# Keys a step ahead of queries in the attention stage of a Performer and mixture-of-experts kernel

## The chip, the cores and the metric

The kernel runs on one core of a Trainium2 chip. The metric is the device time of one execution in microseconds. Engines are named as in the profile: PE (TensorE; PEld is its loading of weights), DVE (VectorE), ACT (ScalarE), POOL (GpSimd), and SP, whose queue issues DMAs.

## The reference

Three layers in a row. The first is Performer attention over 2 batches, 8 heads, 576 positions and 64 dimensions with 128 random features; its output, 1152 rows of 512, goes through four experts, and then through `h * cos(h)` between two matrices. The change lies in the first:

```python
def phi(x):
    proj = np.einsum('bhsd,md->bhsm', x, omega)
    sq = np.sum(x * x, axis=-1, keepdims=True) / 2.0
    h = proj - sq
    h = h - np.max(h, axis=-1, keepdims=True)
    return np.exp(h) / np.sqrt(m)
q_p, k_p = phi(q * scale), phi(k * scale)
kv = np.einsum('bhsm,bhsd->bhmd', k_p, v)
z = np.sum(k_p, axis=2)
num = np.einsum('bhsm,bhmd->bhsd', q_p, kv)
den = np.einsum('bhsm,bhm->bhs', q_p, z)[..., None] + 1e-06
return num / den
```

## The kernel before

Attention is worked in eight steps, one for each batch and pair of heads, over the first 512 positions; the last 64 positions of all heads and both batches form a tail (`kL`, `qL`) of their own. One step `s` turns k and q (PE transposes them in `turn`, and a copy brings them back to SBUF), projects them on the features (`features`: eight matmuls `pj`, which write two banks, the two heads of the pair on the two halves of PE's rows), and takes the exponentials. The exponential's bias is minus the norm term minus the maximum. POOL squares the input and adds up to eight partial sums for each row (`norms`), DVE sums these (`sq`), takes the maximum of each of the eight projections of a row (`mx`), and forms the bias in two operations with two inputs each (`bias`, line 984). ACT applies the eight exponentials of a pair (line 1010).

Around it, `kv_of` multiplies the key features with v and adds the tail's part, `turn_phi` transposes the query features and copies them back (`pT`), `nums` multiplies them with kv and divides, and `put_x` transposes the result and splits it in a high and a low half: ACT writes the high half `xh`, DVE the low half `xl`. `kv_tail` makes the tail's part `kvL` for all heads once.

Each engine takes its instructions in the order of the program. The loop over `s` writes that order out by hand; in step `s` it is: kv of step s-1; projection of k and, in part, its bias; norms on POOL for the next k and q; transposes of the query features of s-1; bias and exponentials of k; result of s-2; projection and bias of q; transposes of the next k and q; num of s-1; loads for later steps; one piece of a weight load. The exponentials of q stand at the start of the next step. A weight unit of the expert layer is loaded in every step from 0 on, two steps later split in a high half by ACT (line 129) and a low half by POOL (line 134). From `s = 6` on, `dense_quanta` puts four quanta of six dense matmuls in a step, for the expert layer; they run on to the end of the kernel. All PSUM tiles come from one pool of eight banks.

Of the kernel before, what the change touches and what calls it, by code (L numbers as in the profile page):

```python
# [26 lines left out]
def performer_moe_kernel(ctx, tc, q, k, v, omega, probs, w1, w2, w_in, w_out, out):  # L27
# [846 lines left out]
    with tc.tile_pool(name="at1", bufs=1) as at1, tc.tile_pool(name="at2", bufs=2) as at2:  # L874
# [51 lines left out]
        ws = at1.tile([P, M], F32, name="ws")  # L926

# [8 lines left out]
        def norms(nm, t):  # L936

            x2 = at2.tile([P, 2 * R, D], F32, tag=f"x2{nm[0]}", bufs=1, name=f"x2_{nm}")
            nc.gpsimd.tensor_tensor(out=x2, in0=t, in1=t, op=ALU.mult)
            sq = at2.tile([P, 2 * R], F32, tag="sq", name=f"sq_{nm}")  # L940
            w = D
            while w > 8:
                w //= 2
                nc.gpsimd.tensor_tensor(
                    out=x2[:, :, 0:w], in0=x2[:, :, 0:w], in1=x2[:, :, w : 2 * w], op=ALU.add
                )
            yield
            nc.vector.tensor_reduce(out=sq, in_=x2[:, :, 0:w], op=ALU.add, axis=AX.X)
            yield sq

        def turn(nm, t, pieces=1):

            n = R // pieces
            tps = []
            for z in range(pieces):
                tp = bank(f"tp_{nm}_{z}")[:, : n * P]
                tps.append((slice(z * n * P, (z + 1) * n * P), tp))
                for i in range(n):
                    nc.tensor.transpose(
                        tp[:, i * P : (i + 1) * P], t[:, 2 * (z * n + i) : 2 * (z * n + i) + 2, :], ident  # L960
                    )

            def copy(x=None):
                if x is None:
                    x = at2.tile([P, R * P], F32, tag=f"xT{nm[0]}", name=f"xT_{nm}")
                for z, (c, tp) in enumerate(tps):
                    if z == (nm[0] == "q"):
# [7 lines left out]
        def features(nm, turned, phi, hold=False):  # L975

            norm = next(sqs.pop(nm))
            mx = at2.tile([P, 2 * R], F32, tag="mx", name=f"mx_{nm}")
            nb = at2.tile([P, 2 * R], F32, tag="nb", name=f"nb_{nm}")
            pjs, rs = [], []  # L980

            def bias(z):
                for dst, o in ((mx, ALU.add), (nb, ALU.subtract)):
                    nc.vector.scalar_tensor_tensor(
                        out=dst[:, z], in0=norm[:, z], scalar=-SC * SC / 2, in1=mx[:, z], op0=ALU.mult, op1=o
                    )

            pjs = [bank(f"pj_{nm}_{g}") for g in range(2)]
            for i in range(R):
                for g, pj in enumerate(pjs):  # L990
                    r = slice(g * D, (g + 1) * D)
                    nc.tensor.matmul(
                        pj[:, i * M : (i + 1) * M], turned[r, i * P : (i + 1) * P], ws[r, :], start=True, stop=True
                    )
            for g, pj in enumerate(pjs):
                rs.append(slice(g, 2 * R, 2))
                nc.vector.tensor_reduce(
                    out=mx[:, rs[-1]], in_=pj.rearrange("p (a m) -> p a m", m=M), op=ALU.max, axis=AX.X
                )
                if nm in ("kL",) and not g:  # L1000
                    bias(rs[-1])

            if hold:
                yield
            bias(rs[-1] if nm in ("kL",) else slice(0, 2 * R))
# [51 lines left out]
        def kv_tail(phi):  # L1057
            for hp in range(NP):
# [6 lines left out]
                nc.scalar.activation(kvL[hp].rearrange("p h b e -> p h (b e)"), kvp, ACTF.Copy)  # L1065
# [15 lines left out]
        def turn_phi(i):  # L1081
            phq = phqs[i]
            for h in range(2):
# [4 lines left out]
                if h == 0:  # L1088
# [65 lines left out]
        def load(i):  # L1154
            b, hp = pairs[i]
            kts[i] = load_pair(k, b, hp, "kt")
            qts[i] = load_pair(q, b, hp, "qt")

        load(0)
        load_tail(halves(kL), k)  # L1160
        load(1)
        load_v(0)
        load_tail([veL[b * L : (b + 1) * L, :, b, 0:D] for b in range(B)], v)
# [23 lines left out]
        def norms_ahead(nm, t):  # L1187
            sqs[nm] = norms(nm, t)
            next(sqs[nm])

        DQ = 1.0
        wload = []
        norms_ahead("k0", kts[0])
        norms_ahead("q0", qts[0])
        fk = fq = iter(())
        turned = {}

        def turn_ahead(s):
            splits = []
            if s == 0:  # L1200
                omega_pairs()
            if s < NPR and ("k", s) not in turned:
                splits.append(("k", turn(f"k{s}", kts[s], 2 if s == 0 else 1)))
            if s == 0:
                warm(1)
            splits.append(("q", turn(f"q{s}", qL if s == NPR else qts[s])))
            if s == 0:
                warm(1)
            for x, split in splits:
                turned[x, s] = split()  # L1210

        def query_features(s):
            phqs[s] = at1.tile([P, 2 * R, M], F32, tag="phq", name=f"phq_{s}")
            steps = features(f"q{s}", turned.pop(("q", s)), phqs[s])
            next(steps)
            return steps

        turn_ahead(0)

        xkL = at1.tile([P, R * P], F32, tag="phq", name="xkL")  # L1220
        for s in range(NPR + 3):
            for _ in fq:
                pass
            if s < first:
                advance(wload)
            dense_quanta(s, DQ)
            kvs = kv_of(s - 1) if 1 <= s <= NPR else iter(())
            next(kvs, None)
            if s != 1:
                next(kvs, None)  # L1230
            if s >= first:
                advance(wload)
            dense_quanta(s, DQ)
            fk = iter(())
            if s < NPR:
                phks[s] = at1.tile([P, 2 * R, M], F32, tag="phk", name=f"phk_{s}")
                fk = features(f"k{s}", turned.pop(("k", s)), phks[s], 1 <= s < first)
                next(fk)
            if s == 0:

                turned["kL"] = turn("kL", kL)(xkL)
                fq = query_features(0)
                norms_ahead("kL", kL)
                k1 = turn("k1", kts[1])
                for _ in fk:
                    pass
                turned["k", 1] = k1()
                phiL = at1.tile([P, H, M], F32, name="phiL")
                fL = features("kL", turned.pop("kL"), phiL)
                next(fL)  # L1250
            if s == 1:
                turn_phi(0)
                kv_tail(phiL)
                next(kvs, None)
            if s + 1 < NPR:
                norms_ahead(f"k{s + 1}", kts[s + 1])
            if s < NPR:
                norms_ahead(f"q{s + 1}", qL if s + 1 == NPR else qts[s + 1])
            dense_quanta(s, DQ)
            if not 1 <= s < first:  # L1260
                next(fk, None)
            if 2 <= s <= NPR:
                turn_phi(s - 1)
            elif s == NPR + 1:
                tail_turn_phi()
            for _ in fk:
                pass
            px = iter(())
            if 2 <= s <= NPR + 1:
                b, hp = pairs[s - 2]  # L1270
                px = put_x(f"{s - 2}", hp, xss.pop(s - 2), b * R, R)
            elif s == NPR + 2:
                px = tail_put_x()
            next(px, None)
            if s == 0:
                for _ in fq:
                    pass
            else:
                fq = query_features(s) if s <= NPR else iter(())
            for _ in px:  # L1280
                pass
            dense_quanta(s, DQ)
            if s < NPR:
                turn_ahead(s + 1)
            if s == 0:
                for _ in fL:
                    pass
            if 1 <= s <= NPR:
                nums(s - 1)
            elif s == NPR + 1:  # L1290
                tail_nums()
            if s + 2 < NPR:
                load(s + 2)
            if s + 1 < NPR:
                load_v(s + 1)
# [51 lines left out]
```

## Time and profile before

| | |
|---|---|
| median of 3 runs | 656.53 us (656.46 to 657.21) |
| the profiled execution | 656.99 us |
| its span, first to last instruction | 655.2 us |
| busy in the span: PE, DVE, ACT, POOL | 648.6, 492.9, 356.8, 173.7 us |
| attention's first eight steps begin, and its last transposes lie | from 6 to 103 us |

The span is what the trace covers; the rest of the execution's time lies around it. PE's matmuls are pipelined and their ends modelled, so the rows of PEld show better when PE goes on. Rows of the timeline merge equal instructions that follow each other; the difference of two starts tells more than a duration, because an instruction may start before the one ahead has ended.

### The profile page before, as it was taken

Reading aid. Unit: us, or ns where it says so; the run is one execution under the profiler, and the core shown is the slowest. Engines: PE = TensorE matmul, PEld = TensorE weight load, DVE = VectorE, ACT = ScalarE, POOL = GpSimd, SP = SyncE. Lnnn points to the kernel's source line nnn. Section 1 sums busy time; section 2 is a strip of 40 time slices with the busy share of each in tenths; the row PEclk is TensorE's granted clock in tenths of the full one; section 3 lists DMA queues with packets and bytes.
Section 4 is the critical chain, followed back from the end, with each engine's and each line's share of the span. In section 5 each row is a group of like instructions: output and inputs, shape, how many; then the busy total and the mean of one; then the engine's idle time right before and its main releaser. Section 6 shows DMA issues by size and latency. Waiting matters only on the chain. (4 is left out here: it accounts for less than half of the span.)

```text
span 655.2 us, 9580 instructions
## 1 busy us (share of the span) xinstructions
PE 648.6 (99%) x3479; PEld 561.1 (86%) x3479; DVE 492.9 (75%) x898; ACT 356.8 (54%) x708; POOL 173.7 (27%) x223
## 2 busy tenths in 40 slices
PE   8999999999999999999999999999999999999997
PEld 7999998998888888888888888788999888888887
DVE  5897749778879778679788587699688677596842
ACT  5887664436544555254544344464476874467921
POOL 8898451203332222333333222320000000000000
PEclk9999999999999999999999999999999999999999
DMA  7753121323544534345543255410811001700111
GB/s 185 221 155 105 34 65 32 97 65 113 154 141 156 176 113 145 128 133 164 187 129 128 99 159 178 144 59 8 319 34 34 1 0 39 284 1 2 48 49 49
DMA packets 55439, 70.93 MB, mean 108 GB/s; under 512 B 15200, under 2 KB 40032, under 8 KB 55392
## 3 DMA queue, kind: packets, MB, share of 16 engines
q1 hardware_dynamic: 46800, 40.92, 20.6%
q0 software_dynamic: 8448, 29.37, 12.9%
q8 instruction: 27, 0.44, 0.3%
q14 instruction: 20, 0.16, 0.1%
q10 hardware_dynamic: 144, 0.03, 0.0%
HBM read 55.36 MB, written 14.94 MB: 107 GB/s over the span
## 5 line engine op out<-in xcount | busy, mean ns | idle before, releaser
L674 ACT ACTIVATE sth<-h 128x512 fp32r<-128x512 f32 (+1 forms) x114 | 61.2, 551 | 69.0 <-PE g L704 54.1
L248 POOL TENSOR_TENSOR c<-c 128x512 uint32<-128x512 uint32 x32 | 47.1, 1472 | 86.6 <-issue 36.3
L677 DVE SCALAR_TENSOR_TENSOR stl<-h,sth 128x512 fp32r<-128x512 f32 (+1 forms) x72 | 49.1, 701 | 25.1 <-ACT sth L674 24.7
L704 PE MATMUL g<-v2h,sth 128*128 128x512 f32 (+1 forms) x110 | 42.6, 387 | 0.4 <-ACT sth L674 0.4
L704 PE MATMUL g<-v3h,sth 128*128 128x512 f32 (+1 forms) x110 | 42.9, 390 | 0.0
L704 PE MATMUL g<-v1h,sth 128*128 128x512 f32 (+1 forms) x110 | 42.7, 388 | 0.0
L704 PE MATMUL g<-v0h,sth 128*128 128x512 f32 (+1 forms) x110 | 42.6, 387 | 0.0
L704 PE MATMUL g<-v0h,stl 128*128 128x512 f32 (+1 forms) x110 | 42.6, 387 | 0.0
L704 PE MATMUL g<-v2h,stl 128*128 128x512 f32 (+1 forms) x110 | 42.5, 387 | 0.0
L704 PE MATMUL g<-v3h,stl 128*128 128x512 f32 (+1 forms) x110 | 42.4, 386 | 0.0
L704 PE MATMUL g<-v1h,stl 128*128 128x512 f32 (+1 forms) x110 | 42.4, 386 | 0.0
L704 PE MATMUL g<-v0l,sth 128*128 128x512 f32 (+1 forms) x110 | 42.4, 385 | 0.0
L704 PE MATMUL g<-v1l,sth 128*128 128x512 f32 (+1 forms) x110 | 42.4, 385 | 0.0
L704 PE MATMUL g<-v3l,sth 128*128 128x512 f32 (+1 forms) x110 | 42.4, 385 | 0.0
L704 PE MATMUL g<-v2l,sth 128*128 128x512 f32 (+1 forms) x110 | 42.4, 385 | 0.0
L282 DVE TENSOR_TENSOR stl<-h,sth 128x512 fp32r<-128x512 f32 (+1 forms) x42 | 24.4, 588 | 21.1 <-ACT sth L674 20.7
L403 DVE SCALAR_TENSOR_TENSOR c<-c 128x384 f32<-128x384 f32 (+2 forms) x44 | 25.8, 590 | 9.0 <-ACT c L401 8.8
L233 ACT ACTIVATE c<-c 128x512 f32<-128x512 f32 x32 | 21.1, 659 | 15.6 <-DMA kv_0h<-c 6.5
L401 ACT ACTIVATE c<-c 128x384 f32<-128x384 f32 (+2 forms) x44 | 24.4, 555 | 1.4
L704 PEld LDWEIGHTS g<-v2h,sth 128*128 128x128 f32 x110 | 20.7, 188 | 4.8 <-ACT sth L674 0.8
L704 PEld LDWEIGHTS g<-v0h,stl 128*128 128x128 f32 x110 | 20.7, 188 | 4.8 <-DVE stl L677 0.4
L704 PEld LDWEIGHTS g<-v2h,stl 128*128 128x128 f32 x110 | 20.7, 188 | 4.6 <-DVE stl L677 0.4
(415 smaller groups left out, 1930.5 us busy)
## 6 DMA issues: line engine op xcount, KB each, us to landing
rv<-in_moe_w_dram SPq DMA_DIRECT2D x16, 512.0 KB, 3.9
c<-in_moe_w_in_dram POOLq DMA_DIRECT2D x16, 512.0 KB, 4.2
c<-in_moe_w_out_dram POOLq DMA_DIRECT2D x16, 512.0 KB, 3.9
kt<-in_k_dram SPq DMA_DIRECT2D x8, 256.0 KB, 3.8
qt<-in_q_dram SPq DMA_DIRECT2D x8, 256.0 KB, 3.7
ve<-in_v_dram SPq DMA_DIRECT2D x16, 128.0 KB, 2.6
ra_2as<-in_moe_w_dram SPq DMA_DIRECT2D x8, 256.0 KB, 2.9
ra_3as<-in_moe_w_dram SPq DMA_DIRECT2D x8, 256.0 KB, 3.7
```

The lines of the kernel that those rows point to most:

```text
L233: nc.scalar.activation(t.bitcast(F32), hw.bitcast(F32), ACTF.Abs)
L248: nc.gpsimd.tensor_tensor(out=total, in0=t, in1=lw, op=ALU.add)
L282: nc.vector.tensor_tensor(out=dst, in0=x, in1=y, op=ALU.subtract)
L401: nc.scalar.activation(kk, vv, ACTF.Copy, bias=ROUND)
L403: nc.vector.scalar_tensor_tensor(out=vv, in0=kk, scalar=ROUND, in1=vv, op0=ALU.subtract, op1=ALU.subtract)
L674: nc.scalar.activation(hi, src, ACTF.Relu if self.e < E else ACTF.Copy)
L677: nc.vector.scalar_tensor_tensor(out=to, in0=src, scalar=0.0, in1=hi.bitcast(F32), op0=ALU.max, op1=ALU.subtract)
L704: nc.tensor.matmul(g, x, y[:, o : o + w], start=n == 0, stop=n == 3 * FT - 1)
```

## The change

The order of the loop changes: in step `s` the queries of `s` and the keys of `s+1` are projected one after the other, then both biases are formed, then both exponentials taken, and the next q and the k after it are turned. So keys run a step ahead; k is loaded three steps ahead, q two. The start is written out by hand for k0, q0, the tail's keys, k1, and the loop's step 0 only loads. The bias is formed by operations with one input: a sum over the eight partial norms, its scaling into a plane of a small tile `three`, the maxima into another, and two sums over the planes. For the tail's keys the norm is no longer POOL's and DVE's: ACT writes the squares beside the copy of the turned keys, and eight further matmuls add them, times a constant, into the projection, so that the negated maximum is the bias. Some copies pass from ACT to DVE (`kvL`, `pT` of step 0, one turned k). Buffers: two for `phk` and for the norms' `x2`; `xkL` and `x2L` use the places of `pT`.

```diff
-        def norms(nm, t):
+        def norms_ahead(nm, t):
...
-            yield
-            nc.vector.tensor_reduce(out=sq, in_=x2[:, :, 0:w], op=ALU.add, axis=AX.X)
-            yield sq
+            sqs[nm] = x2[:, :, 0:w]
...
+                    if x2 is not None:
+                        nc.scalar.activation(x2[:, c], tp, ACTF.Square)
...
-            def bias(z):
-                for dst, o in ((mx, ALU.add), (nb, ALU.subtract)):
-                    nc.vector.scalar_tensor_tensor(
-                        out=dst[:, z], in0=norm[:, z], scalar=-SC * SC / 2, in1=mx[:, z], op0=ALU.mult, op1=o
-                    )
...
+                for z, (x_, y) in enumerate([(turned, ws)] + [(squares, minus_norm)] * (squares is not None)):
+                    for g, pj in enumerate(pjs):
+                        r = slice(g * D, (g + 1) * D)
+                        nc.tensor.matmul(
+                            pj[:, i * M : (i + 1) * M], x_[r, c], y[r, :],
+                            start=z == 0, stop=z == (squares is not None),
+                        )
+            yield
+            three = at2.tile([P, 2 * R, 3], F32, tag=f"th{nm[0]}", name=f"three_{nm}")
+            if squares is None:
+                nc.vector.tensor_reduce(out=nb, in_=sqs.pop(nm), op=ALU.add, axis=AX.X)
+                nc.vector.tensor_scalar(
+                    out=three[:, :, 1], in0=nb, scalar1=-SC * SC / 2, scalar2=None, op0=ALU.mult
+                )
             for g, pj in enumerate(pjs):
+                to = (nb if squares is not None else three[:, :, 0])[:, g : 2 * R : 2]
                 nc.vector.tensor_reduce(
+                    out=to, in_=pj.rearrange("p (a m) -> p a m", m=M), op=ALU.max, axis=AX.X,
+                    negate=squares is not None,
                 )
+            if squares is None:
+                nc.vector.tensor_reduce(
+                    out=three[:, :, 2], in_=three[:, :, 0:2], op=ALU.add, axis=AX.X, negate=True
+                )
+                nc.vector.tensor_reduce(out=nb, in_=three[:, :, 1:3], op=ALU.add, axis=AX.X)
             yield
...
-                nc.scalar.activation(kvL[hp].rearrange("p h b e -> p h (b e)"), kvp, ACTF.Copy)
+                nc.vector.tensor_copy(out=kvL[hp].rearrange("p h b e -> p h (b e)"), in_=kvp)
...
-                if h == 0:
+                if h == 0 and i:
...
+        load_k(2)
         load_tail([veL[b * L : (b + 1) * L, :, b, 0:D] for b in range(B)], v)
...
+        norms_ahead("k0", kts[0])
+        norms_ahead("q0", qts[0])
+        norms_ahead("k1", kts[1])
+        omega_pairs()
+        k0 = turn("k0", kts[0], 2)
+        warm(1)
+        q0 = turn("q0", qts[0])
+        warm(1)
+        turned["k", 0], turned["q", 0] = k0(), q0()
...
+        fk0 = k_features(0)
+        next(fk0)
+        kL_copy = turn("kL", kL)
+        next(fk0)
+        kL_copy(xkL, x2L)
+        k1 = turn("k1", kts[1])
+        for _ in fk0:
+            pass
+        turned["k", 1] = k1()
+        fq0 = q_features(0)
+        next(fq0)
+        fL = features("kL", xkL, phiL, x2L)
+        next(fL)
+        next(fq0)
+        next(fL)
+        norms_ahead("q1", qts[1])
+        norms_ahead("k2", kts[2])
+        turn_ahead(1, act=False)
+        fk1 = k_features(1)
+        next(fk1)
+        for _ in fq0:
+            pass
+        for _ in fL:
+            pass
+        for _ in fk1:
+            pass
...
+        for s in range(NPR + 3):
             if s == 0:
+                load_k(3)
+                load_q(2)
+                load_v(1)
+            else:
+                if s < first:
+                    advance(wload)
+                dense_quanta(s, DQ)
+                kvs = kv_of(s - 1) if s <= NPR else iter(())
                 next(kvs, None)
+                if s == 1:
+                    turn_phi(0)
+                    kv_tail(phiL)
+                next(kvs, None)
+                if s >= first:
+                    advance(wload)
+                dense_quanta(s, DQ)
+                if 2 <= s <= NPR:
+                    turn_phi(s - 1)
+                elif s == NPR + 1:
+                    tail_turn_phi()
+                px = iter(())
+                if 2 <= s <= NPR + 1:
+                    b, hp = pairs[s - 2]
+                    px = put_x(f"{s - 2}", hp, xss.pop(s - 2), b * R, R)
+                elif s == NPR + 2:
+                    px = tail_put_x()
+                next(px, None)
+                for _ in px:
                     pass
+                fs = []
+                if s <= NPR:
+                    fs.append(q_features(s))
+                if s + 1 < NPR:
+                    fs.append(k_features(s + 1))
+                for f in fs:
+                    next(f)
+                for f in fs:
+                    next(f)
+                dense_quanta(s, DQ)
+                for f in fs:
+                    for _ in f:
+                        pass
+                if s + 1 <= NPR:
+                    norms_ahead(f"q{s + 1}", q_of(s + 1))
+                if s + 2 < NPR:
+                    norms_ahead(f"k{s + 2}", kts[s + 2])
+                turn_ahead(s + 1)
+                dense_quanta(s, DQ)
+                if s <= NPR:
+                    nums(s - 1)
+                elif s == NPR + 1:
+                    tail_nums()
+                if s + 3 < NPR:
+                    load_k(s + 3)
+                if s + 2 < NPR:
+                    load_q(s + 2)
+                if s + 1 < NPR:
+                    load_v(s + 1)
             advance(wload)
```

## Rows read from the trace of the kernel before

**Rows 1.** The page: busy time by engine; granted clock by slice.
```profile
PE 648.6 (99%) x3479; PEld 561.1 (86%) x3479; DVE 492.9 (75%) x898; ACT 356.8 (54%) x708; POOL 173.7 (27%) x223
...
PEclk9999999999999999999999999999999999999999
```
**Rows 2.** Waits of PE's weight loads: total, times, longest, in us.
```profile
PEld kvL L1061 <- ACT phiL L1010: 2.0, 1, 2.0
PEld pj_q L992 <- issue: 1.3, 8, 0.2
```
**Rows 3.** Timeline of PE's weight loads, step 2: start, us, instruction, count.
```profile
22.65 1.87 PEld L1073 LDWEIGHTS kv<-ve,phk 128*128 128x128 f32 x16
24.58 0.97 PEld L992 LDWEIGHTS pj_k<-ws,xT_k 64*128 64x128 f32 x16
25.67 0.86 PEld L1086 LDWEIGHTS tq<-ident,phq 128*128 128x128 f32 x8
...
28.23 0.42 PEld L959 LDWEIGHTS tp_k<-ident,kt 128*128 128x128 f32 x4
...
30.83 1.87 PEld L1073 LDWEIGHTS kv<-ve,phk 128*128 128x128 f32 x16
```
**Rows 4.** The same in step 6, between dense quanta (g).
```profile
56.93 1.93 PEld L1073 LDWEIGHTS kv<-ve,phk 128*128 128x128 f32 x16
...
60.03 0.97 PEld L992 LDWEIGHTS pj_k<-ws,xT_k 64*128 64x128 f32 x16 [0.25 <-issue]
61.12 0.19 PEld L503 LDWEIGHTS g<-xh,w02h 128*128 128x128 f32 x1
```
**Rows 5.** Timeline of ACT: exponentials of k0.
```profile
9.26 2.17 ACT L1010 ACTIVATE phk<-pj_k,nb_k 128x128 f32<-128x128 f32 x8 [0.60 <-DVE nb_k L984]
```
**Rows 6.** Timeline of ACT in step 3.
```profile
36.54 2.17 ACT L1010 ACTIVATE phk<-pj_k,nb_k 128x128 f32<-128x128 f32 x8 [1.33 <-DVE nb_k L984]
38.55 0.71 ACT L1046 ACTIVATE xh<-tx 128x384 fp32r<-128x384 f32 x2
39.08 0.67 ACT L968 ACTIVATE xT_k<-tp_k 128x512 f32<-128x512 f32 x1
39.56 1.14 ACT L129 ACTIVATE w1h<-ra_2p 128x1024 fp32r<-128x1024 f32 x1
40.50 2.25 ACT L1010 ACTIVATE phq<-pj_q,nb_q 128x128 f32<-128x128 f32 x8
```
**Rows 7.** Timeline of PE's weight loads: the tail's kv products.
```profile
16.96 1.87 PEld L1061 LDWEIGHTS kvL<-veL,phiL 128*128 128x128 f32 x16 [1.97 <-ACT phiL L1010]
```
**Rows 8.** Timeline of DVE, steps 2 and 3: maxima and two-input sums.
```profile
25.78 1.29 DVE L997 TENSOR_REDUCE mx_k<-pj_k 128x4 f32<-128x512 f32 x2 [0.66 <-PE pj_k L992]
...
36.28 0.17 DVE L984 SCALAR_TENSOR_TENSOR nb_k<-sq_k,mx_k 128x8 f32<-128x8 f32 x1
...
37.98 1.03 DVE L984 SCALAR_TENSOR_TENSOR mx_q<-sq_q,mx_q 128x8 f32<-128x8 f32 x1
```
**Rows 9.** DVE's groups, 20 to 125 us: busy us, mean ns; idle before.
```profile
L1024 DVE RECIPROCAL rd<-rd 128x4 f32<-128x4 f32 x16 | 2.1, 168 | 0.0
...
L948 DVE TENSOR_REDUCE sq_q<-x_q 128x8 f32<-128x64 f32 x7 | 1.5, 209 | 0.0
```
**Rows 10.** Timeline of ACT and DVE around a result's split.
```profile
30.51 0.71 ACT L1046 ACTIVATE xh<-tx 128x384 fp32r<-128x384 f32 x2
...
31.25 0.76 DVE L1048 TENSOR_TENSOR xl<-tx,xh 128x384 fp32r<-128x384 f32 x2 [0.58 <-ACT xh L1046]
...
31.92 0.68 DVE L970 COPY xT_q<-tp_q 128x512 f32<-128x512 f32 x1
```
**Rows 11.** Timeline of PE: the tail's num products and last transposes.
```profile
96.62 1.95 PE L1130 MATMUL numL<-kv,pTL 128*128 128x130 f32 x16
...
102.53 0.60 PE L1034 MATMUL tx_L<-ident,xsL 128*128 128x128 f32 x4
```
**Rows 12.** Timeline of DVE: the tail's division.
```profile
99.54 2.46 DVE L1143 TENSOR_TENSOR xsL<-numL,rdL 64x128 f32<-64x128 f32 x8
```

More of the change, by code (lines that the diff above doesn't have):

```diff
@@ L926, in performer_moe_kernel @@
         ws = at1.tile([P, M], F32, name="ws")
+        minus_norm = at1.tile([P, M], F32, name="minus_norm")
+        nc.gpsimd.memset(minus_norm, -SC * SC / 2)
         def omega_pairs():
@@ L934, in performer_moe_kernel @@
         sqs = {}
-        def norms(nm, t):
-            x2 = at2.tile([P, 2 * R, D], F32, tag=f"x2{nm[0]}", bufs=1, name=f"x2_{nm}")
+        def norms_ahead(nm, t):
+            x2 = at2.tile([P, 2 * R, D], F32, tag=f"x2{nm[0]}", name=f"x2_{nm}")
             nc.gpsimd.tensor_tensor(out=x2, in0=t, in1=t, op=ALU.mult)
-            sq = at2.tile([P, 2 * R], F32, tag="sq", name=f"sq_{nm}")
             w = D
@@ L961, in turn, with copy @@
                     )
-            def copy(x=None):
+            def copy(x=None, x2=None, act=True):
                 if x is None:
@@ L966, in copy @@
                 for z, (c, tp) in enumerate(tps):
-                    if z == (nm[0] == "q"):
+                    if act and z == (nm[0] == "q"):
                         nc.scalar.activation(x[:, c], tp, ACTF.Copy)
@@ L970, in copy @@
                         nc.vector.tensor_copy(out=x[:, c], in_=tp)
-                return x
-            return copy
[L975 to L980, printed above, removed]
-            def bias(z):
-                for dst, o in ((mx, ALU.add), (nb, ALU.subtract)):
-                    nc.vector.scalar_tensor_tensor(
-                        out=dst[:, z], in0=norm[:, z], scalar=-SC * SC / 2, in1=mx[:, z], op0=ALU.mult, op1=o
-                    )
+                    if x2 is not None:
+                        nc.scalar.activation(x2[:, c], tp, ACTF.Square)
@@ L988, in features @@
+                return x
+            return copy
+        def features(nm, turned, phi, squares=None):
+            nb = at2.tile([P, 2 * R], F32, tag=f"nb{nm}"[:3], name=f"nb_{nm}")
             pjs = [bank(f"pj_{nm}_{g}") for g in range(2)]
             for i in range(R):
[L990 to L994, printed above, removed]
+                c = slice(i * P, (i + 1) * P)
+                for z, (x_, y) in enumerate([(turned, ws)] + [(squares, minus_norm)] * (squares is not None)):
[12 more added lines that the diff above has]
+                )
@@ L995, in features @@
             for g, pj in enumerate(pjs):
-                rs.append(slice(g, 2 * R, 2))
+                to = (nb if squares is not None else three[:, :, 0])[:, g : 2 * R : 2]
                 nc.vector.tensor_reduce(
-                    out=mx[:, rs[-1]], in_=pj.rearrange("p (a m) -> p a m", m=M), op=ALU.max, axis=AX.X
-                )
[L1000 to L1005, printed above, removed]
+                    out=to, in_=pj.rearrange("p (a m) -> p a m", m=M), op=ALU.max, axis=AX.X,
+                    negate=squares is not None,
+                )
@@ L1151, in tail_put_x, with load_k, load_q @@
                 yield from put_x(f"L{hp}", hp, xs[:, hp : hp + 1, :, :], NTILE - 1, 1)
-        def load(i):
+        def load_k(i):
             b, hp = pairs[i]
             kts[i] = load_pair(k, b, hp, "kt")
+        def load_q(i):
+            b, hp = pairs[i]
             qts[i] = load_pair(q, b, hp, "qt")
-        load(0)
+        load_k(0)
+        load_q(0)
         load_tail(halves(kL), k)
-        load(1)
+        load_k(1)
+        load_q(1)
         load_v(0)
+        load_k(2)
         load_tail([veL[b * L : (b + 1) * L, :, b, 0:D] for b in range(B)], v)
@@ L1185, in dense_quanta, with q_of, turn_ahead @@
                 next(stream)
-        def norms_ahead(nm, t):
-            sqs[nm] = norms(nm, t)
-            next(sqs[nm])
         DQ = 1.0
         wload = []
+        turned = {}
+        def q_of(s):
+            return qL if s == NPR else qts[s]
+        def turn_ahead(s, act=True):
+            splits = []
+            if s <= NPR:
+                splits.append((("q", s), turn(f"q{s}", q_of(s))))
+            if s + 1 < NPR:
+                splits.append((("k", s + 1), turn(f"k{s + 1}", kts[s + 1])))
+            for key, split in splits:
+                turned[key] = split(act=act)
@@ L1193, in performer_moe_kernel, with k_features, q_features @@
+        def k_features(s):
+            phks[s] = at2.tile([P, 2 * R, M], F32, tag="phk", name=f"phk_{s}")
+            return features(f"k{s}", turned.pop(("k", s)), phks[s])
+        def q_features(s):
+            phqs[s] = at1.tile([P, 2 * R, M], F32, tag="phq", name=f"phq_{s}")
+            return features(f"q{s}", turned.pop(("q", s)), phqs[s])
         norms_ahead("k0", kts[0])
         norms_ahead("q0", qts[0])
[L1195 to L1199, printed above, removed]
-            if s == 0:
[L1201 to L1229, printed above, removed]
-                next(kvs, None)
[L1231 to L1245, printed above, removed]
-                    pass
[L1247 to L1283, printed above, removed]
-                turn_ahead(s + 1)
[L1285 to L1295, printed above, removed]
@@ new lines, in performer_moe_kernel @@
+        norms_ahead("k1", kts[1])
[5 more added lines that the diff above has]
+        turned["k", 0], turned["q", 0] = k0(), q0()
+        xkL = at2.tile([P, R * P], F32, tag="pT0", bufs=1, name="xkL")
+        x2L = at2.tile([P, R * P], F32, tag="pT1", bufs=1, name="x2L")
+        phiL = at1.tile([P, H, M], F32, name="phiL")
+        fk0 = k_features(0)
+        next(fk0)
+        kL_copy = turn("kL", kL)
+        next(fk0)
```

2 lines of the change are left out of this document (added).

## The prediction

> **What bounds the kernel now.** I read the page first. PE is busy 648.6 of 655.2 us, its weight loads apart no other engine over 75%, and the granted clock is full in every slice [rows 1]: what counts is when PE stands still, and how much it has to do. So next comes the list of waits, for PE's weight loads, since PE takes its instructions in order. One wait is long: the tail keys' kv products stand 2.0 us for the exponentials of `phiL`. The other item to see is "issue", 1.3 us over eight projections, 0.16 each [rows 2]. Then the timeline of PE's weight loads over one step before the dense work starts (s = 2): kv, projection, transposes, projection, transposes, num follow with no gap worth the name, and kv comes back after 30.83 - 22.65 = 8.18 us [rows 3]. PE's work sets these steps; what the change rewrites is the order of ACT and DVE beside it. From s = 6 dense quanta come between [rows 4], and PE stays full to the end. So a change here can win the 2 us, win switches of PE, or lose by stalling PE in steps 2 to 5, where no dense work covers it; what PE has gained or lost by the kv of step 6 is carried to the end.
>
> **The parts, on PE.** Added: eight matmuls on the squares of the tail keys, the size of one projection, 0.97 us of weight loads. Removed: stretches of projections. A projection alone in steps 2 to 5 takes 25.67 - 24.58 = 1.09 us against 0.97 for its loads, with up to 0.06 ahead [rows 3]; among dense quanta, 61.12 - 60.03 + 0.25 = 1.34 [rows 4]. Two in one stretch save 0.12 to 0.18 a step early and 0.37 late. A step without stalls is then 8.18 - 0.18 = 8.0 us. Moved: by the kv of step 6 the new order has already projected k6 (1.34) and turned k7 (0.41, half of the 0.82 below), and q6 with k7 will save 0.37: what remains is 2.12 us shorter. I compare both kernels at that kv, which starts at 56.93 now [rows 4].
>
> **The start.** In ACT's new order the exponentials of k0 (now at 9.26 [rows 5]) are followed by the copy of k1, then those of q0, kL and k1. Eight exponentials take 2.01 us from start to start, a copy 0.48 [rows 6]: 9.26 + 2.01 + 0.48 + 2 x 2.01, and the last one's tail, end `phiL` near 16.0, against an end that now lets the tail's kv start at 16.96 [rows 7]. PE has the squares, tp_k2 and k1 to do meanwhile. The tail's kv: 16.2 to 18.1. Then q1 and k2 in one stretch from 18.4. The first maximum starts 1.2 us after a stretch starts (24.58 to 25.78 [rows 3, 8]), so 19.6; two maxima 1.29 and two small sums 0.42 [rows 8, 9] and the hand-over 0.09 give the first q bias of the loop, b1 = 21.4. PE meanwhile: stretch 2.07, transposes and num 30.83 - 28.23 = 2.60 [rows 3], so the next kv at 18.4 + 2.07 + 2.60 = 23.1, against 22.65, with 1.5 us of later work done. To here the change is about 1.1 us ahead, its squares paid.
>
> **Steps 2 to 5: a loop through ACT and DVE.** Now the queues. In the new order ACT runs, from the q bias of a step: exponentials of q, of the next k, copy of the turned k, the high half of a weight unit (one a step, ends of steps 1 to 4), and in the next step `pT` and `xh`. DVE's `xl` waits for `xh`, and behind `xl` in DVE's queue stand the norm sum, the two maxima and the three sums that make the next q bias, for which ACT waits again. Now, the k maxima and the `pT` copy are ahead of that and run while ACT is busy. The loop, from starts: exponentials 2 x 2.01 (36.54 to 38.55), copy 0.48, weight 0.94 (39.56 to 40.50) [rows 6], `pT` 0.48 (as the other copy of 512), `xh` to `xl` 0.74 (30.51 to 31.25), `xl` 0.67 [rows 10], norm sum 0.21 and its scaling 0.15, maxima 1.29, two sums 2 x 0.21 [rows 8, 9], hand-over 0.09 (36.28 + 0.17 to 36.54 [rows 6, 8]): 9.5 us. PE needs 8.0. So the loop, not PE, would set these steps, though the two-input sums go: they took 0.17 us at best and 1.03 at worst [rows 8], but they were not what PE waited for.
> Unknown in it: the sums over 8 x 2, taken as the reduce of 8 x 8 (0.21; at least the 0.17 of the shortest sum [rows 8]), and the scaling from SBUF. For that the nearest row of one input is the reciprocal, 0.17 on average over 16 [rows 9]; the other bound is the longest two-input sum, 1.03 [rows 8]. I take the short end, since it too has one input. Overlap of the small ones could take off 0.3, so the loop lies between 9.2 and, with a slow scaling, 10.4.
> The Trainium skill, "SBUF — State Buffer", section "Who interferes with whom", says that a reduce never contends with GpSimd, but that a scalar operation from SBUF may enter a mode that takes the port pair both share. Were the new scaling held like the longest two-input sum, a loop would grow by 0.88 us and the total by 2.6; no trace here shows it.
>
> **The sum.** The q bias of step 4 is b1 + 3 x 9.5 = 49.9. PE's stretch of step 5 waits for the turned k, 2 x 2.01 + 0.67 [rows 6] and the 0.16 of issue after it: 54.75; stretch 2.07, transposes and num 2.60, a dense quantum 0.98 (kv's 1.87 of loads after 56.93, up to 60.03 - 0.25 [rows 3, 4]): kv at 60.4, where PE alone would be at 23.1 + 4 x 8.0 + 0.98 = 56.1. Against now: 60.4 - 56.93 - 2.12 = +1.35. From step 6 a step has four quanta, PE work of about 12 us, and the loop is covered.
> At the end of the stage one more: the tail's transposes come after two quanta behind its num products, not three. Now numL ends at 98.57 and the transposes start at 102.53, 1.32 a quantum [rows 11]; `xsL` is done at 102.0 [rows 12]. Two quanta end at 101.2, and the last of four transposes waits: 0 to 0.9, I take 0.6.
> Sum: +1.95 us on a profiled 656.99 (span 655.2 and 1.8 around it), which is 0.46 above the median of 656.53. On the median: 658.5. Three moves I cost at nothing. The early load of k2 goes through SP's queue ahead of the tail's v, which PE wants only with the tail's kv at 16; later k loads go out a step sooner, behind reads of their buffers that are long over. POOL's norms come a step ahead of their use, and POOL has one set fewer, the tail's; the bias waits for them only if POOL falls a whole step behind, and then each microsecond goes into the loop. DVE takes over the tail's four kv copies and one `pT` copy: they end with the tail's kv, while PE projects q1 and k2.
>
> **Rivals.** (1) The loop is shorter than PE's 8.0, because more of DVE's small work overlaps than the starts show: kv at 56.1, so 56.1 - 56.93 - 2.12 + 0.6 = -2.35, or 654.2. It decides at a loop of 8.4 (total = 3 x loop - 26.55). For it: PE has no wait in steps 2 to 5 now. Against: every link is a queue in order or data. (2) Loop 8.4 to 9.3, within 0.2% (1.3 us, about what a measurement of this kernel can tell from no change): 655.3 to 657.8. (3) The loop as said, and a bank for the kv of step 6 comes free only with the first q exponentials: 1.1 more, 659.6; the waits of now show no such wait. (4) The clock falls to its lower level of 1.2 GHz in the stalls of 1.5 us: for one step of 8.0 that is 8 us more, 666. The longest stall now, 2.0 us, left it full [rows 1, 2].
> The Trainium skill, "TensorE: Matmul & The Clock Gate", section "HAM oscillation", warns that PE's idle gaps lower the clock; no slice here shows it.
>
> **Chances.** Slower 0.58: the forecast 0.42 (own range 657.8 to 660.5), rival 3 and the slow scaling 0.14, rival 4 0.02. Same 0.20: rival 2. Faster 0.22: rival 1, mostly 653.5 to 655. Range 653.9 to 661.2: it cuts the lower half of rival 1 and the top of the slow cases.
>
> **What would show it.** Right: after step 2, ACT idle about 3 us a step between `xh` and the q exponentials, released by the bias; DVE idle before `xl`; PE idle 1 to 1.5 us in steps 3 to 5, a kv period near 9.5; the kv of step 6 near 60.4; `kvL` no longer waiting 2 us. Wrong: a kv period of 8.0 to 8.2 with PE full there, or a start that reaches the kv of step 2 more than 0.5 us off 23.1.

## The result and the profile after

The changed kernel takes 663.47 us (median of six runs, 661.57 to 666.39) against 656.99 for the kernel before beside it: a ratio of 1.0097, interval 1.0068 to 1.0125, so about 1% slower. 658.5 was forecast, with 661.2 as the top of the range: the sign was right, the size was not. The profiled execution took 663.72 us with a span of 661.9, against 656.99 and 655.2: 6.7 us more to explain.

The page, busy time by engine and granted clock by slice, to be read against [rows 1]: PE has 16 matmul records more and is busy 3.2 us longer, and two slices, from 33 to 66 us, have lost clock.

```profile
PE 651.8 (98%) x3495; PEld 565.5 (85%) x3495; DVE 495.6 (75%) x916; ACT 355.5 (54%) x703; POOL 170.7 (26%) x220
...
PEclk9988999999999999999999999999999999999999
```

The waits of PE's weight loads (us in total, times, longest). The 2.0 us for `phiL` of [rows 2] are gone; the kv products now stand three times for the exponentials of q, 4.5 us in all: 0.31 in the start, then 2.04 and 2.18. Not one wait after the start is for a turned k.

```profile
PEld kv L1074 <- ACT phq L1011: 4.5, 3, 2.2
```

The timeline of PE's weight loads: tail's kv, then the kv of steps 2 to 6, and the dense quantum (g) ahead of the last. [rows 3] had a step of 8.2 us; here kv comes after 10.0, 11.0, 10.6 and 11.0. At 32.50 the same 16 loads take 3.49 us instead of 1.87.

```profile
15.93 1.87 PEld L1062 LDWEIGHTS kvL<-veL,phiL 128*128 128x128 f32 x16
22.54 1.87 PEld L1074 LDWEIGHTS kv<-ve,phk 128*128 128x128 f32 x16
32.50 3.49 PEld L1074 LDWEIGHTS kv<-ve,phk 128*128 128x128 f32 x16 [2.04 <-ACT phq L1011]
43.49 1.86 PEld L1074 LDWEIGHTS kv<-ve,phk 128*128 128x128 f32 x16
54.14 1.86 PEld L1074 LDWEIGHTS kv<-ve,phk 128*128 128x128 f32 x16 [2.18 <-ACT phq L1011]
...
64.14 0.19 PEld L503 LDWEIGHTS g<-xh,w02h 128*128 128x128 f32 x1 [0.47 <-ACT phq L1011]
...
65.18 1.88 PEld L1074 LDWEIGHTS kv<-ve,phk 128*128 128x128 f32 x16
```

The timeline of ACT, the exponentials of q; a round is the time from one of these starts to the next. ACT is idle for 2.5 to 3.3 us before each, for the bias: by DVE's timeline the second sum of the q bias ends 0.1 us before each start, also where the view names another operation that ends at about that time.

```profile
21.30 2.18 ACT L1011 ACTIVATE phq<-pj_q,nb_q 128x128 f32<-128x128 f32 x8 [2.52 <-DVE nb_q L1006]
31.31 2.18 ACT L1011 ACTIVATE phq<-pj_q,nb_q 128x128 f32<-128x128 f32 x8 [3.29 <-DVE nb_k L992]
42.30 2.18 ACT L1011 ACTIVATE phq<-pj_q,nb_q 128x128 f32<-128x128 f32 x8 [2.86 <-DVE nb_q L1006]
52.94 2.18 ACT L1011 ACTIVATE phq<-pj_q,nb_q 128x128 f32<-128x128 f32 x8 [3.29 <-DVE nb_k L992]
62.95 2.18 ACT L1011 ACTIVATE phq<-pj_q,nb_q 128x128 f32<-128x128 f32 x8 [3.20 <-PE num L1103]
```

The timeline of DVE ahead of the second of them. `xl` waits for `xh`, and the whole chain to the bias stands behind it, as the prediction had it. The scaling, L993, is 0.63 us long.

```profile
28.05 0.76 DVE L1049 TENSOR_TENSOR xl<-tx,xh 128x384 fp32r<-128x384 f32 x2 [1.90 <-ACT xh L1047]
28.72 0.21 DVE L992 TENSOR_REDUCE nb_q<-x_q 128x8 f32<-128x64 f32 x1
28.96 0.63 DVE L993 TENSOR_SCALAR three_q<-nb_q 128x8 f32<-128x8 f32 x1
29.51 1.28 DVE L998 TENSOR_REDUCE three_q<-pj_q 128x4 f32<-128x512 f32 x2
30.82 0.17 DVE L1003 TENSOR_REDUCE three_q<-three_q 128x8 f32<-128x16 f32 x1
31.02 0.17 DVE L1006 TENSOR_REDUCE nb_q<-three_q 128x8 f32<-128x16 f32 x1
```

POOL's timeline in the same stretch, and the tile view of `three_q` (ns: least, median, most). POOL's operation on the weight ends at 29.56, the scaling at 29.59. The same operation takes 173 ns at best, 535 at the median, 966 at worst; the two sums always take 170.

```profile
27.06 2.50 POOL L134 TENSOR_TENSOR w02l<-ra_0p,w02h 128x512 fp32r<-128x512 f32 x2 [3.96 <-DMA ve<-in_v_dram]
29.52 1.05 POOL L941 TENSOR_TENSOR x_q<-qt 128x512 f32<-128x512 f32 x1
```
```profile
L993 DVE TENSOR_SCALAR three_q<-nb_q x9: 173/535/966, 9.7 to 93.8; 128x8 f32<-128x8 f32 x9
L1003 DVE TENSOR_REDUCE three_q<-three_q x9: 169/170/171, 11.7 to 95.2; 128x8 f32<-128x16 f32 x9
```

The view by windows (us; busy PE, PEld, DVE, ACT, POOL; granted clock; DMA share; GB/s). PE stands still from 31 to 32.5, and the clock is then 0.50, the lower level of 1.2 GHz, for over 6 us. A second, shorter fall follows at 56 us (0.54 from 56 to 58, 0.50 to 59.5).

```profile
31.00:32.50 1.50, 0.00 (x0) 0.00 (x0) 1.44 (x5) 1.19 (x5) 1.34 (x4) 0.92 1.04 312
32.50:36.00 3.50, 3.50 (x17) 3.50 (x18) 2.32 (x11) 3.50 (x14) 2.29 (x4) 0.50 0.45 140
36.00:38.60 2.60, 2.60 (x13) 2.34 (x12) 0.96 (x2) 1.58 (x3) 1.54 (x2) 0.50 0.55 130
```

Where the 6.7 us came from, by PE's weight loads, with the same points read in the trace of before: the kv of step 6 starts 65.18 - 56.93 = 8.25 later; from there to `numL` (102.56, before 96.44) it is 37.38 us against 39.51, -2.13; from `numL` to the last stage's first dense loads, behind the tail's transposes (122.41, before 115.01), 19.85 against 18.57, +1.28; the rest of the span 539.49 against 540.19, -0.70. Sum: +6.7. Up to the kv of step 2 the change was 0.1 us ahead; all of the loss lies between it and the kv of step 6, and in the tail.

### The profile page after: what moved, and what is told of

It reads as the page before. It is cut to its first block, busy times and chain, and to the rows that moved or that the text cites. A ratio compares the mean times of both kernels' runs of the same rounds, so it can differ in the third digit from the quotient of the medians.

```text
span 661.9 us, 9631 instructions
## 1 busy us (share of the span) xinstructions
PE 651.8 (98%) x3495; PEld 565.5 (85%) x3495; DVE 495.6 (75%) x916; ACT 355.5 (54%) x703; POOL 170.7 (26%) x220
## 4 chain that ended last, share of the span: by engine, by line
PE 86%; DVE 6%; ACT 3%; issue 2%; DMA 1%; POOL 1%; ACTq 0%; DVEq 0%; POOLq 0%
PE g L704 43%; PE g L503 5%; PE g_odd L533 3%; PE g_0a L503 2%; PE g_0c L503 2%; PE g_3a L503 2%; PE g_2a L503 2%; PE g_1a L503 2%; PE g_2c L503 2%; PE g_3c L503 2%; PE g_1c L503 2%; PE kv L1074 2%; PE g_0b L503 1%; PE g_0e L503 1%; PE g_0d L503 1%
## 5 line engine op out<-in xcount | busy, mean ns | idle before, releaser
L1011 ACT ACTIVATE phq<-pj_q,nb_q 128x128 f32<-128x128 f32 x72 | 19.6, 383 | 24.6 <-DVE nb_q L1006 14.7
L232 ACT ACTIVATE c<-c 128x512 f32<-128x512 uint32 x32 | 21.3, 666 | 8.5 <-DMA c<-in_moe_w_in_dram 7.5
```

The lines of the kernel that those rows point to most:

```text
L232: nc.scalar.activation(lw.bitcast(F32), lw, ACTF.Copy, bias=2.0, scale=2.0**-51)
L1011: nc.scalar.activation(phi[:, ix, :], pj[:, i * M : (i + 1) * M], ACTF.Exp, bias=nb[:, ix : ix + 1])
```

## The experiments

Theory A: the round of the queues (q bias, ACT's exponentials and copies, `xh`, `xl`, maxima, sums, next bias) sets steps 2 to 5, with the clock on top. B: the round is long mainly because the scaling is held while POOL works. C: the clock is the main loss. D, a rival to A's price once `xl` is out of the way: a bank that only the q exponentials free closes a round of its own through PE.

**e1: `xh` and `xl` behind both biases.**

```diff
                 next(px, None)
-                for _ in px:
-                    pass
                 fs = []
...
                 for f in fs:
                     next(f)
+                for _ in px:
+                    pass
                 dense_quanta(s, DQ)
```

> The changed kernel with one move: the splits of the result (xh on ACT, xl on DVE) are emitted behind both biases instead of ahead of them, so that the bias no longer stands behind xl in DVE's queue; the scaling with one input, the banks and all counts stay. Theory A (a loop ACT, xh, xl, maxima, bias, ACT of about 10 us sets steps 2 to 5, and the fallen clock comes on top): the loop is cut, q bias to q bias 8.0 to 8.4 us, PE stalls in steps 2 to 5 under 1 us in all, clock full, kv of step 6 near 56, total 654.5 to 656. Theory B (the scaling held by GpSimd is what makes the loop long): it stays, so 661 to 664. Theory C (the clock that falls is the main loss, the stall only its trigger): a stall is still there, 660 to 664.

Measured: 657.70 us (656.85 to 659.61, ten runs), ratio 1.0015 (1.0001 to 1.0028): one move of one loop gives back about 5.8 us, though A's 654.5 to 656 is missed. The rounds, by ACT's timeline, are now 7.7, 9.0, 8.9 and 10.1 us:

```profile
29.00 2.18 ACT L1011 ACTIVATE phq<-pj_q,nb_q 128x128 f32<-128x128 f32 x8 [0.99 <-DVE nb_k L992]
38.00 2.18 ACT L1011 ACTIVATE phq<-pj_q,nb_q 128x128 f32<-128x128 f32 x8 [2.09 <-DVE nb_k L992]
46.91 2.18 ACT L1011 ACTIVATE phq<-pj_q,nb_q 128x128 f32<-128x128 f32 x8 [2.06 <-DVE nb_q L1006]
57.05 2.18 ACT L1011 ACTIVATE phq<-pj_q,nb_q 128x128 f32<-128x128 f32 x8 [2.25 <-DVE nb_k L992]
```

A is right on the place, not on the rounds (8.0 to 8.4) or on PE's stall. The scaling now meets more of POOL's work (DVE's timeline), and PE's num waits for the exponentials of q, 2.6 us in four times (waits of PE's weight loads):

```profile
34.75 0.21 DVE L992 TENSOR_REDUCE nb_q<-x_q 128x8 f32<-128x64 f32 x1
34.99 1.30 DVE L993 TENSOR_SCALAR three_q<-nb_q 128x8 f32<-128x8 f32 x1
```
```profile
PEld num L1103 <- ACT phq L1011: 2.6, 4, 0.9
```

After the longest of these, 0.85 us at 48.1, the clock falls to 0.59 from 50 to 53; that this wait is the cause is not shown. The runs part by the clock: five with a mean of 1.0 took 656.85 to 657.51 us, five with 0.997 took 657.89 to 659.61.

**e2: the scaling done by POOL, inside the partial norms.** DVE's sum writes its plane directly.

```diff
+            nc.gpsimd.tensor_scalar(
+                out=x2[:, :, 0:w], in0=x2[:, :, 0:w], scalar1=-SC * SC / 2, scalar2=None, op0=ALU.mult
+            )
             sqs[nm] = x2[:, :, 0:w]
...
-                nc.vector.tensor_reduce(out=nb, in_=sqs.pop(nm), op=ALU.add, axis=AX.X)
-                nc.vector.tensor_scalar(
-                    out=three[:, :, 1], in0=nb, scalar1=-SC * SC / 2, scalar2=None, op0=ALU.mult
-                )
+                nc.vector.tensor_reduce(out=three[:, :, 1], in_=sqs.pop(nm), op=ALU.add, axis=AX.X)
```

> The changed kernel with the scaling of the norms moved from DVE to GpSimd (one operation more on its 128x64 partial sums), so that DVE goes from the norm sum straight to the maxima. Theory A: the loop loses the 0.5 us that the scaling was held, 9.4 to 9.6 us from q bias to q bias where the clock is full, PE still stalls over 1 us a step, total 660.5 to 662.5. Theory B: the loop falls to PE's 8.0 to 8.3 and the total to 655 to 657. Theory C: 662 to 664, or less only if the clock stays full.

Measured: 662.08 us (660.86 to 665.12), ratio 1.0091 (1.0057 to 1.0126). ACT's timeline shows rounds of 9.33, 9.49, 9.33 and 9.43 us from a start at 21.20:

```profile
30.53 2.17 ACT L1011 ACTIVATE phq<-pj_q,nb_q 128x128 f32<-128x128 f32 x8 [2.63 <-DVE nb_q L1006]
40.02 2.17 ACT L1011 ACTIVATE phq<-pj_q,nb_q 128x128 f32<-128x128 f32 x8 [2.64 <-DVE nb_q L1006]
```

That is the forecast loop, 9.5, less its 0.15 for the scaling, within 0.15: together the other links were priced right, and B is only a part. The clock still falls (0.83 from 30 to 40 us), which takes part of the gain.

**e3: PE kept busy.** In steps 2 to 5 eight products of zeros go to columns of `num` that nothing reads.

```diff
                 parts.append((num, xs[:, :, h, :]))
+            if 1 <= i <= 4:
+                for _ in range(8):
+                    nc.tensor.matmul(num[:, 3 * P : 4 * P], zero, zero, start=True, stop=True)
             divide(i, parts)
```

> The changed kernel with eight matmuls of zeros into unused columns of the last num bank in each of steps 2 to 5, where PE would stand still, so that it has work while it waits; they add nothing to any result. Theory A: the clock stays full from 20 to 70 us, q bias to q bias is 10.0 us in all four rounds of the loop instead of 10.0 to 11.0, and the total 660.5 to 662: the clock is worth 1.5 to 2.5 us of 6.5. Theory B: the same, since the scaling is not touched. Theory C: the total falls to 656 to 658. If the matmuls themselves delay PE, it is slower than the changed kernel.

Measured: 661.61 us (661.35 to 662.03), ratio 1.0069 (1.0049 to 1.0090). The view by windows has the full clock where it had fallen (from 50 to 60 us too):

```profile
30.00:40.00 10.00, 10.00 (x104) 9.56 (x103) 7.53 (x26) 6.70 (x21) 7.51 (x12) 1.00 0.48 134
```

The q exponentials start at 21.51, 31.77, 41.75, 51.74 and 61.74: rounds of 10.0 to 10.3 with the clock full, so C is out as the main cause. ACT's timeline has the fifth of them, and PE's weight loads the kv of step 6 behind it:

```profile
61.74 2.17 ACT L1011 ACTIVATE phq<-pj_q,nb_q 128x128 f32<-128x128 f32 x8 [3.20 <-DVE nb_k L992]
```
```profile
62.93 0.19 PEld L503 LDWEIGHTS g<-xh,w02h 128*128 128x128 f32 x1 [0.29 <-ACT phq L1011]
...
63.96 1.88 PEld L1074 LDWEIGHTS kv<-ve,phk 128*128 128x128 f32 x16
```

By the medians the clock was worth 663.47 - 661.61 = 1.9 us, and the spread of the runs shrinks from 4.8 us to 0.7.

**e4: the one-input sums alone, in the kernel before.** The order is that of before; the bias is formed as in the change, with the scaling ahead of the maxima.

```diff
-            def bias(z):
-                for dst, o in ((mx, ALU.add), (nb, ALU.subtract)):
-                    nc.vector.scalar_tensor_tensor(
-                        out=dst[:, z], in0=norm[:, z], scalar=-SC * SC / 2, in1=mx[:, z], op0=ALU.mult, op1=o
-                    )
+            nc.vector.tensor_scalar(
+                out=three[:, :, 1], in0=norm, scalar1=-SC * SC / 2, scalar2=None, op0=ALU.mult
+            )
+            def bias(z):
+                nc.vector.tensor_reduce(
+                    out=three[:, z, 2], in_=three[:, z, 0:2], op=ALU.add, axis=AX.X, negate=True
+                )
+                nc.vector.tensor_reduce(out=nb[:, z], in_=three[:, z, 1:3], op=ALU.add, axis=AX.X)
```

> The kernel before with one part of the change alone: the bias is summed by operations with one input (scaling, two sums over planes) in place of the two with two inputs; order, buffers and norms stay. Theory A: PE still sets the step, kv to kv 8.2 us, total 656 to 657.5, no difference that can be measured. Theory B: the scaling is held in this order too and sits ahead of the maxima, so ACT's wait for the k bias grows and the total is 658 or more.

Measured: 657.88 us (656.65 to 658.13, ten runs), ratio 1.0003 (0.9991 to 1.0016): no difference that can be measured, though the median lies 0.4 above A's range. By PE's weight loads two things cancel. The start gains: `kvL` no longer waits (15.28 instead of 16.96 [rows 7]), so most of the 2.0 us of [rows 2] was the price of the two-input sums, and the kv of step 2 comes 0.9 us earlier (21.76). From there to step 6 the kernel loses 1.1 us: the scaling is held here too, up to 1.24 us ahead of the maxima, num waits twice for the exponentials of k (0.27 and 0.16), and kv comes after 8.2, 8.4, 8.9 and 10.0 us, where before has 8.2, 8.3, 8.2 and 9.5. So B is right that the scaling is held and costs here too, and the total does not show it.

**e5: e1 and e2 together.**

> Both earlier moves in one kernel: the result's splits behind the biases (as in the first experiment) and the scaling on GpSimd (as in the second). Theory A: with the loop through xl cut, the scaling, held up to 1.3 us in the first experiment, is what is left ahead of the maxima; without it q bias to q bias is 7.7 to 8.3 us in all four rounds, PE does not stall over 1 us in a piece, the clock stays full from 20 to 60 us, and the total is 655 to 656.5. Rival D (the wait of num for a bank of the q projection, seen in the first experiment, closes a loop of its own of about 9 us whatever DVE does): q bias to q bias stays at 8.7 to 9, total 657 to 658.

Measured: 656.84 us (656.09 to 657.32, ten runs), ratio 0.9995 (0.9986 to 1.0004): level with before, at full clock. The rounds are 7.84, 8.49, 8.48 and 8.48 us, between the 8.3 that A would have and D's 8.7. The rows for why stand with e6, which has the same steps.

**e6: e5, and one dense quantum of the last step moved ahead of the tail's transposes.**

```diff
                 elif s == NPR + 2:
+                    dense_quanta(s, DQ)
                     px = tail_put_x()
...
-                dense_quanta(s, DQ)
+                if s < NPR + 2:
+                    dense_quanta(s, DQ)
```

> As the kernel with both moves, and in the last step one dense quantum is put ahead of the tail's transposes in place of the one behind them, so that three quanta stand between the tail's num products and its transposes as in the kernel before. Theory A: the 1.3 us that PE stands at these transposes go, total 0.7 to 1.4 below the kernel with both moves, 654 to 655.5, below the kernel before by 0.2% or more. If the stall at the transposes is not covered by a third quantum, no difference from the kernel with both moves.

Measured: 655.35 us (655.25 to 655.84, eight runs), ratio 0.9971 (0.9961 to 0.9981): 0.3% faster than before and 8.1 us faster than the change as it was made. It is the version to keep. From `numL` to the last stage's first dense loads it is 19.03 us, where e5 has 20.40 and the kernel before 18.57. One round of steps 3 and 4, first ACT, then PE's weight loads, then DVE and ACT again:

```profile
37.67 2.18 ACT L1011 ACTIVATE phq<-pj_q,nb_q 128x128 f32<-128x128 f32 x8 [1.77 <-DVE nb_q L1006]
...
46.16 1.15 ACT L1011 ACTIVATE phq<-pj_q,nb_q 128x128 f32<-128x128 f32 x4 [1.77 <-DVE nb_q L1006]
```
```profile
38.87 0.97 PEld L1103 LDWEIGHTS num<-kv,pT 128*128 128x128 f32 x8 [0.42 <-ACT phq L1011]
39.91 1.86 PEld L1074 LDWEIGHTS kv<-ve,phk 128*128 128x128 f32 x16
...
43.15 0.97 PEld L988 LDWEIGHTS pj_q<-ws,xT_q 64*128 64x128 f32 x16 [0.17 <-issue]
```
```profile
44.35 1.29 DVE L998 TENSOR_REDUCE three_q<-pj_q 128x4 f32<-128x512 f32 x2 [0.71 <-PE pj_q L988]
...
45.87 0.17 DVE L1006 TENSOR_REDUCE nb_q<-three_q 128x8 f32<-128x16 f32 x1
```

The round closes through PE: exponentials to the second half of num 1.20, num to kv 1.04, kv to the projection 3.24, projection to maximum 1.20, maximum to the next exponentials 1.81: 8.49 us, of which PE stands 0.42 ahead of num. So PE's own work is 8.07, near the 8.0 of the prediction, and D is the mechanism that is left, at a smaller price than it was given. It is read from starts and releasers; no run took the bank wait away.

**e7: only the dense quantum moved, in the change as made.** The diff is that of e6.

> The changed kernel with only the dense quantum of the last step put ahead of the tail's transposes. Theory A: steps 2 to 5 as in the changed kernel (q bias to q bias 10 to 11 us, the clock falling), the tail's transposes without their stall of 1.3 us: 661.5 to 663. If PE's stall at the transposes is made up for later anyway, 663 to 664.

Measured: 660.52 us (660.22 to 665.00, five runs), ratio 1.0064 (1.0040 to 1.0088). That is below either forecast. From `numL` to the last stage's first dense loads it is 18.56 instead of 19.85, what before has (18.57): -1.29, the tail's stall. The profiled execution also reached the kv of step 6 at 64.01, 1.2 earlier, its clock having fallen less; that is not the edit's.

**e8: e6 with the tail's norms back on POOL and DVE, without the squares.**

```diff
+        norms_ahead("kL", kL)
         norms_ahead("k1", kts[1])
...
-        kL_copy(xkL, x2L)
+        kL_copy(xkL)
...
-        fL = features("kL", xkL, phiL, x2L)
+        fL = features("kL", xkL, phiL)
```

> The kernel with all three moves, with the tail keys' norms put back on GpSimd and DVE (a norm set between those of q0 and k1, no squares on ACT, no eight matmuls on squares), so that this part of the change is undone alone. Theory A: PE saves 0.97 us of matmuls, but phiL waits for the later bias, the tail's kv starts 0.5 to 1.5 us later and the first q bias of the loop with it; in all 0 to 1 us above the kernel with all three. If the squares only cost PE time, 0.5 to 1 us below it.

Measured: 658.58 us (658.01 to 659.28, ten runs), ratio 1.0020 (1.0008 to 1.0032): 3.2 above e6, where 0 to 1 was expected. The start is late: ACT's first exponentials of q at 23.52 instead of 21.35, and by PE's weight loads the kv of step 2 at 24.82 instead of 22.93.

```profile
19.58 0.52 PEld L1062 LDWEIGHTS kvL<-veL,phiL 128*128 128x128 f32 x4 [1.20 <-DVE pT L1092]
...
24.82 1.87 PEld L1074 LDWEIGHTS kv<-ve,phk 128*128 128x128 f32 x16
```

So the squares earn more than their eight products cost: 2.1 us at the last stage's first dense loads (116.41, in e6 114.29). Another 1.4 us of e8's loss lies after that point. The waits of PE's weight loads show where: in the last stage they stand 1.5 us for `stl` of DVE and 0.9 for `sth` of ACT, in e6 not at all. All three kernels with the tail's norms on POOL (before, e4, e8) take 540.2 to 540.8 us from the first dense loads of that stage to the end, all seven without 539.0 to 539.5. Why is not shown.

## Why the prediction failed where it did

**Right: the place, and the start but for 0.06 us.** `kvL` came at 15.93 (16.2 forecast), the first q bias at 21.3 (21.4), the kv of step 2 at 22.54 (23.1): 0.56 early, just over the 0.5 that the prediction itself had named as a sign of being wrong. Half of it is `kvL`; 0.2 more is the gap that was put between the tail's kv and the stretch behind it without a row. From step 3 on ACT and DVE stand as described, and e1 shows that `xl` ahead of the bias was the link. One reading did not hold: that PE had not been waiting for the two-input sums is true of steps 2 to 5, not of the 2.0 us at `kvL`, as e4 shows. What remained behind that stage was 2.13 us shorter, forecast 2.12.

**The step that failed** is "Steps 2 to 5: a loop through ACT and DVE" with its end in "The sum": the kv of step 6 was put at 60.4 and came at 65.18, 4.8 us later. There PE was to wait 1 to 1.5 us a step for the turned k, ahead of the projections. It waits ahead of kv instead, for the exponentials of q, 2.04 and 2.18 us in two of the steps, so the kv of step 6 hangs on the fifth q bias and not on the fourth. Three terms make up the 4.8; e3, whose clock stays full, separates them.

1. The scaling, taken at its short end, 0.15. Its median is 0.535, and e3's rounds are 10.26, 9.98, 9.99 and 10.0 instead of 9.5: the fifth q exponentials at 61.74 instead of 59.4, +2.3. About 1.8 of that is the scaling: by e3's timeline of DVE it is 0.46 to 0.54 from its start to that of the maxima in each round, and in the first round a held scaling also put the exponentials of k off by 0.33. The start gives 0.1, and other links run about 0.1 a round over their prices. e2 without the scaling on DVE has 9.33 to 9.49. The nearest row by number of inputs was the reciprocal [rows 9], which is never long in the kernel before (150 to 179 ns, 16 times); the longest two-input sum [rows 8] was the better guide. The Trainium skill, "SBUF — State Buffer", section "Who interferes with whom", says that such a scalar operation can take the port pair that DVE shares with GpSimd, and a reduce never does. The rows agree: 173 to 966 ns for the one, 169 to 171 for the other, and the end of the scaling falls with the end of POOL's operation.
2. The bank, rival 3. The dense quantum ahead of that kv waits for the exponentials of q, so kv comes 2.2 us after the fifth of them starts, not 1.0, in the change and in e3 alike: +1.2, where the rival had 1.1. (The wait shows as 0.47 us at 64.14, because PE at the lower clock came late, and as 0.29 in e3, where zeros fill it.) That it is a bank is inferred: neither the quantum nor kv reads `phq`, and no run took the bank wait away. The rival was put aside because the view of waits of before has none for the exponentials of q. But there PE, not the exponentials, set the steps; the wait came with the loop.
3. The clock, rival 4, given 0.02: 65.18 - 63.96 = +1.2 in the profiled execution, 1.9 by the medians of e3 and the change. The falls cost less than the 8 us of the rival, because the first lasts under 7 us and the second about 3.4, and PE would have stood for part of them anyhow. The ground for putting the rival aside, a stall of 2.0 us at full clock, was one profile: of the 44 runs of the kernel before beside the experiments 11 have a mean clock of 0.997 and took 657.2 to 659.3 us, the others 655.7 to 657.8. The Trainium skill, "TensorE: Matmul & The Clock Gate", section "HAM oscillation", warns that idle gaps of PE lower the clock, in an example with longer gaps than these. The runs agree: the six runs of the change go from 661.57 at a mean clock of 0.995 to 666.39 at 0.989.

**The tail** was mis-sized: +1.28 for a forecast 0.6, of which e7 gets back all. Three of the four transposes wait in turn (timeline of PE's weight loads), where before they came together [rows 11]:

```profile
107.05 0.14 PEld L1035 LDWEIGHTS tx_L<-ident,xsL 128*128 128x128 f32 x1
107.57 0.14 PEld L1035 LDWEIGHTS tx_L<-ident,xsL 128*128 128x128 f32 x1 [0.38 <-PE tx_L L1035]
108.19 0.14 PEld L1035 LDWEIGHTS tx_L<-ident,xsL 128*128 128x128 f32 x1 [0.48 <-ACT xh L1047]
108.81 0.14 PEld L1035 LDWEIGHTS tx_L<-ident,xsL 128*128 128x128 f32 x1 [0.48 <-PE tx_L L1035]
```

DVE's timeline says why. The prediction let `xsL` follow `numL` as it does before, 2.92 us from start to start [rows 11, 12]; here it is 3.50 (PE's `numL` begins at 102.74), behind an operation of 1.54 us ahead of it in the queue. The transposes then go at the pace of the division, 2.46 / 4 = 0.62 us for the two parts that each needs, though the view puts their waits down to others:

```profile
103.76 1.54 DVE L677 SCALAR_TENSOR_TENSOR stl<-c,sth 128x256 fp32r<-128x256 f32 x1 [1.49 <-ACT sth L674]
...
106.24 2.46 DVE L1144 TENSOR_TENSOR xsL<-numL,rdL 64x128 f32<-64x128 f32 x8
```

Against the forecast on the profiled basis, 656.99 + 1.95 = 658.94: +4.78 at the kv of step 6, +0.68 in the tail and -0.70 behind it make the 4.8 that were missing. The -0.70 was not forecast; it lies where e8 has its last 1.4.

**Open.** Which stall lowers the clock and which does not (below); why the last stage is longer with the tail's norms on POOL; and whether another bank would take PE's 0.4 us from e6's round.

## What to carry to other kernels

When an order is written out by hand, add up the round of each in-order queue that waits for another one, and put everything that the next bias does not need behind it: here moving one such operation gave back about 5.8 us of the 6.5, the clock's share of its stalls included, more than all other edits. A stall that a change creates has a second price in the clock, and a third in the banks that are held meanwhile; ask of each stalled engine what it is holding. Where a price has two bounds, do not choose by the number of inputs: look how long each row gets beside a busy POOL. Here the reciprocal and the reduces were never long, the two-input sums and the scaling were.

## What the runs showed of the hardware

The scaling, a 128x8 TENSOR_SCALAR with one input from SBUF, took 0.17 us at best and up to 1.30 (e1), 1.24 (e4) and 0.97 us (the change) beside POOL's work. Where it is long it ends about 0.03 us after an operation of POOL that was running: 29.59 after 29.56, and 43.31 after 43.28. Reduces from SBUF, between the same neighbours, stayed at 0.17 to 0.21.

The clock fell to 1.2 GHz after PE had waited 2.04 us at 32.5 and 2.18 us at 54.1, and in e1 after a wait of 0.85. The second fall and the one in e1 came about 2 us or more after PE had gone on. In the kernel before, PE stood 1.97 us ahead of `kvL` [rows 7] and kept the full clock, by the view by windows:

```profile
15.00:17.00 2.00, 0.24 (x4) 0.04 (x1) 1.97 (x5) 1.21 (x6) 1.92 (x3) 1.00 0.87 221
17.00:20.00 3.00, 3.00 (x32) 2.80 (x32) 2.92 (x8) 2.40 (x8) 2.69 (x6) 1.00 0.90 273
```

The same kernel's runs differ in it, the kernel before included, so one profile's clock is a sample. That makes a kernel with stalls not only slower but less even: 4.8 us between six runs of the change, 0.6 between eight of e6.
